# Plain keys and queries transposed as four 64x64 pieces at a time, into two PSUM banks

## The chip, the cores and the metric

The kernel runs on one NeuronCore of a Trainium2 chip. Its engines each follow their own instruction stream: TensorE (PE in the profile; its weight loads are listed apart as PEld), VectorE (DVE), ScalarE (ACT), GpSimd (POOL) and SyncE (SP). The last two issue most DMAs. The metric is the device time of one launch in microseconds; lower is better. Before the change it is 304.22 us, the median of three runs from 304.19 to 305.46.

## What is computed

Attention over a batch of 8, with 8 heads, 576 positions and 64 numbers a head, and behind it a two-layer network on the 4608 tokens. The first four heads ("plain") look back over a window of 32 positions, the last four ("dilated") over 128 positions, every fourth one.

```python
scores = scale * np.matmul(q, k.transpose(0, 1, 3, 2))
mask_plain = (rel >= 0) & (rel < window)
mask_dil = (rel >= 0) & (rel < window * dilation) & (rel % dilation == 0)
...
attn = np.exp(scores)
attn = attn / (np.sum(attn, axis=-1, keepdims=True) + 1e-09)
out = np.matmul(attn, v)
...
x = attn_out.transpose(0, 2, 1, 3).reshape(B * S, H * D)
h = x @ w_in
g = h * (1.0 / (1.0 + np.exp(-beta * h)))
return g @ w_out
```

Here `rel` is the query's position less the key's, and `w_in` is 512 by 2048.

## The kernel before, in words

**Tiles.** TensorE contracts over the partitions, so keys and queries are needed with the 64 numbers of a head on the partitions: two heads fill 128. The heads thus go in pairs: `x` counts the two plain pairs (`kT[kv][:, x]`, `qT[kv][:, x]`), and head `h` of a pair lies on partitions 64h to 64h+63. The scores of a head are 64-row matmuls on its half (L728), the exponentials go from a PSUM bank into `pt` (L600), multiplied by a mask from batch 1 on (L604), and `pt` is the stationary operand of the value matmuls (L785). The results are normalised on DVE (L619, L620), transposed back (L822, L837, L807) and copied into `xT`. The network works on blocks of 512 tokens: first layer (L868), tanh on ACT (L877), gate on DVE (L882), second layer (L903), eviction (L918, L920), store.

**Where keys and queries come from.** For batches 0, 1 and 2 (`b < DIRECT`) they are loaded position by position and transposed on TensorE; from batch 3 on a DMA transposes them. For the plain heads the staging tile `stp[z]` (`z` 0 for keys, 1 for queries) holds the heads of pair `i`: row 64h + g has nine consecutive positions of head h. One step, named KP0, KP1, QP0 or QP1, transposes one pair: 18 pieces of 64x64 (L473), piece (j, h) from rows of half h to partitions of half h, all into one bank. Then one copy of 128x576 on DVE or ACT (L239) empties the bank into `kT` or `qT`. The dilated steps KD0 to QD1 transpose six blocks of 96x128 each (L466).

**The order of the work** is made when the program is built. `Plan.op` notes every step with its engines, an estimated duration, the steps it needs and a due time `vt`. `Plan.run` then simulates the engines: on each it takes the step that could start first and, among those within 40 to 60 ns of the first (`NEAR`), the one with the earliest due time. A step that needs PSUM takes one of 8 banks (`acquire`), or several at once; `CAPS` limits how many of a kind are open. The instructions are emitted in that order, and each engine keeps to it whatever the chip does. Where the simulation sees TensorE idle it puts in a matmul of zeros as filler (L1015). `NUDGE` moves single steps by hand: its keys are the numbers of the steps in the order in which they are noted, and the value (ns) is added to the step's start when the first is chosen; -900 means that it is taken well ahead of its turn.

Step numbers that matter below: 4 is the zeroing of `pt` and `ptt` (DVE, L317), 7 is `add_d` (POOL, L346: the additive mask of the dilated heads of batch 0), 13 the load of the first keys on SP, 16 to 18 the other loads of keys and queries of batch 0 on POOL, 32 is `ident_f` (POOL, L948), which the transpose of beta (step 33, L951) needs. `add_d` is needed by the four 128x512 matmuls at L654, which start the dilated scores of batch 0.

In `attention`, a pair's transposes and copy are these lines:

```python
g = Group("a")
tr = plan.op([("PE", (18 * mm(64) if kind == "P" else 6 * mm(QT)))],
             lambda e, g=g, z=z, kind=kind, i=i: t_transposes(g, z, kind, i),
             srcs + [ident], vt, acquire=g)
...
steps[n] = [plan.op([dve(S), act(S)], evac, [tr, fill1] + war(key), vt, group=g)]
```

Of the kernel before, what the change touches and what calls it, by code (L numbers as in the profile page):

```python
# [9 lines left out]
BF16 = mybir.dt.bfloat16  # L10
# [26 lines left out]
class Plan:  # L37
# [3 lines left out]

    CAPS = {"h": 3, "p": 4, "o": 2, "z": 4, "a": 8, "s": 5, "w": 6}
    SWITCH = 95
    NUDGE = {32: -900, 54: 400, 98: -900, 188: -60, 192: -150, 263: -400, 287: 400, 292: -400, 294: 60,
        296: -150, 299: -60, 313: 900, 338: -400, 369: -150, 403: 400, 411: 900, 424: 400, 427: -150,
        527: -400, 770: -150, 970: -900, 977: -900, 988: -400, 1057: -60}
    LAT = {"PE": 210, "ACT": 45, "DVE": 45, "POOL": 60, "SP": 0}
    NEAR = {"PE": 40, "ACT": 60, "DVE": 60, "POOL": 60, "SP": 0}

# [3 lines left out]
    def op(self, engs, fn, deps=(), vt=0.0, acquire=None, group=None, dma=0, lat=None, halves=False, sbuf=False):  # L53
        acquire = acquire if acquire is None or isinstance(acquire, list) else [acquire]
        o = Op(engs, fn, deps, vt, acquire, group or acquire, dma, lat, halves, sbuf)
        o.bias = self.NUDGE.get(len(self.ops), 0)
        self.ops.append(o)
# [123 lines left out]
def kernel(  # L181
# [10 lines left out]
    nc = tc.nc  # L192
    P = 128
    B, H, S, D = q.shape
# [11 lines left out]
    GD = S // RD  # L206
    RP = 9
    GP = S // RP
    QT = 96
# [6 lines left out]
    DIRECT = 3  # L216
# [14 lines left out]
    plan = Plan(range(8))  # L231
    E = {"ACT": nc.scalar, "DVE": nc.vector, "POOL": nc.gpsimd}

    def bank(g, dt=FP32):
        b = BANKS[g.bank][:]
        return b if dt == FP32 else b.bitcast(BF16)

    def copy(e, out, in_):
        (nc.scalar.copy if e == "ACT" else E[e].tensor_copy)(out=out, in_=in_)  # L239
# [4 lines left out]
    ident_b = const([P, P], BF16, "ident_b")  # L244
# [28 lines left out]
    st = [const([P, 2 * RD * D + 2 * RP * D], BF16, f"st{i}") for i in range(2)]  # L273
    std = [s[0:2 * GD, 0:2 * RD * D].rearrange("p (x e) -> p x e", x=2) for s in st]
    stp = [s[:, 2 * RD * D:].rearrange("p (x e) -> p x e", x=2) for s in st]
# [16 lines left out]
    mm = lambda n: n / 2.4 + 2.5  # L292
# [14 lines left out]
    ident = plan.op([("POOL", 550)], t_ident, vt=-8.985)  # L307
# [150 lines left out]

    def t_transposes(g, z, kind, i):
        if kind == "D":
            tp = bank(g, BF16)[:, 0:S].rearrange("p (s x g) -> p s x g", s=3, x=2)
            for s_ in range(3):
                for x in range(2):
                    nc.tensor.transpose(tp[:, s_, x], std[z][:, x, (2 * s_ + i) * P:(2 * s_ + i + 1) * P],  # L466
                                        ident_b[0:2 * GD, 0:2 * GD])
        else:
            tp = bank(g, BF16)[:, 0:S].rearrange("p (j g) -> p j g", j=RP)
            for j in range(RP):  # L470
                for h in range(2):
                    rows = slice(64 * h, 64 * h + 64)
                    nc.tensor.transpose(tp[rows, j], stp[z][rows, i, j * D:(j + 1) * D], ident_b[rows, rows])  # L473

    def at_once(x, i, h):

# [5 lines left out]
    def war(*keys):  # L482
        return [o for key in keys for o in last.get(key, ())]

    def used(key, o):
        last.setdefault(key, []).append(o)

    def wrote(*keys):
        for key in keys:
            last[key] = []  # L490
# [38 lines left out]
    def attention(b, ld, names, vts):  # L529
# [2 lines left out]
        vt_of = dict(zip(names, vts))  # L532
        kv = b % 2
        if b < DIRECT:
            for n in [x for x in names if x[0] in "KQ"]:
                z, kind, i = "KQ".index(n[0]), n[1], int(n[2])
                vt = vt_of[n]
                g = Group("a")
                srcs = ld["qk", z, 0 if kind == "P" else 4]
                srcs = srcs if isinstance(srcs, list) else [srcs]  # L540
                tr = plan.op([("PE", (18 * mm(64) if kind == "P" else 6 * mm(QT)))],
                             lambda e, g=g, z=z, kind=kind, i=i: t_transposes(g, z, kind, i),
                             srcs + [ident], vt, acquire=g)
                used(("st", z), tr)
                def evac(e, g=g, z=z, kind=kind, i=i):
                    tp = bank(g, BF16)[:, 0:S]
                    if kind == "P":
                        dst = qT[kv][:, i] if z else kT[kv][:, i, WIN:]
                        copy(e, dst.rearrange("p (g j) -> p g j", j=RP), tp.rearrange("p (j g) -> p g j", j=RP))
                    else:  # L550
                        copy(e, (dk, dq)[z][kv][:, i].rearrange("p h (g s) -> p h g s", s=3),
                             tp.rearrange("p (s h g) -> p h g s", s=3, h=4))
                key = (("kT", "qT")[z], kv, i) if kind == "P" else (("dk", "dq")[z], kv, i)
                steps[n] = [plan.op([dve(S), act(S)], evac, [tr, fill1] + war(key), vt, group=g)]
                wrote(key)
        else:
            ready = {"D": [ld["x", 0, 4], ld["x", 1, 4]], "P": [ld["x", 0, 0], ld["x", 1, 0], fill1]}
# [25 lines left out]
        vt = vt_of["zVAL"]  # L583
# [41 lines left out]
        for name in [n for n in names if n[0] in "ST"]:  # L625
            vt = vt_of[name]
            if name == "T":
                g = Group("s")

                def score(e, g=g):  # L630
                    sc = bank(g)[:, 0:256].rearrange("p (c h r u) -> p h c r u", h=4, c=2, r=2)
                    for h4 in range(4):
# [4 lines left out]
                              deps, vt, acquire=g)  # L637
# [7 lines left out]
            x = int(name[1])  # L645
# [3 lines left out]
            gs = [Group("s") for _ in range(2 * len(xs))]  # L649
            if x >= 2:  # L650
# [7 lines left out]
                def score(e, xs=xs, gs=gs):  # L658
                    for n, x in enumerate(xs):
                        for i in range(4):  # L660
                            r, h4 = i // 2, 2 * (x - 2) + i % 2
                            for c in range(2):
# [7 lines left out]
                              acquire=None if before else gs, group=gs, halves=True)  # L670
# [9 lines left out]
            j = int(name[2])  # L680
            if b >= AT_ONCE:
                if name != "S00":
                    continue
                gs = [Group("w") for _ in range(6)]
# [37 lines left out]
            def score(e, xs=xs, j=j, gs=gs):  # L722
                for n, x in enumerate(xs):
                    for a in range(3):
                        i = 3 * j + a
                        for h in range(2):
# [7 lines left out]
                          vt, acquire=None if before else gs, group=gs, halves=True)  # L734
# [3 lines left out]
            for n, x in enumerate(xs):  # L738
                for h in range(2):
                    exp_and_mask((x, j, h), sop, gs[2 * n + h], vt, 3 * QT,  # L740
                                 lambda g=gs[2 * n + h]: bank(g)[:, 0:3 * QT].rearrange("p (a n) -> p a n", a=3),
                                 lambda x=x, j=j, h=h: pt[x][:, 6 * j:6 * j + 6].rearrange(
                                     "p (a h) n -> p h a n", h=2)[:, h, :, 0:QT],
                                 lambda j=j: mask_n[:, 1 + j:4 + j],
                                 [("pt", x, i) for i in range(3 * j, 3 * j + 3)])
        for name in [n for n in names if n[0] in "VU"]:
            vt = vt_of[name]
            g = Group("a")
# [14 lines left out]
            x, j = int(name[1]), int(name[2])  # L763
# [37 lines left out]
        for name in [n for n in names if n[0] in "XY" and b < BY_DMA]:  # L801
            vt = vt_of[name]
            x = int(name[1])
            g = Group("a")
# [28 lines left out]
            j = int(name[2])  # L833
# [124 lines left out]
    vts = [-3 + 2 * i / len(first) for i in range(len(first))] + [-3, -2.5]  # L958
    vts[first.index("T"):len(first)] = [.2,.35,.45,.5]
    attention(0, ld[0], names0, vts)  # L960

    def xready(lo, hi, kts=range(NKT)):
# [34 lines left out]
    for t in range(NTT):  # L997
# [4 lines left out]
        b = t + 1  # L1002
# [46 lines left out]
```

The softmax here doesn't subtract the row's maximum and nothing guards it: scores larger than these inputs give would overflow.

## Time and profile before

| | |
|---|---|
| time, median of 3 | 304.22 us (304.19 to 305.46) |
| profiled execution: span, first to last instruction | 302.8 us (the page lists no other time of this execution) |
| PE busy | 292.8 us, 97% |
| DVE, ACT, POOL busy | 187.8, 170.3, 88.5 us |
| L473, plain transposes, 216 pieces of 64x64 | busy 4.7 us, one lasts 194 ns; at 10.5 to 13.0, 31.4 to 32.7 and 54.8 to 58.3 us |
| L239, 128x576 copies out of a bank | one lasts about 0.75 us on DVE, 0.64 us on ACT |
| L868 and L903, the network's matmuls of 128x512 | 134.7 and 132.9 us busy |

Matmuls are pipelined: one that lasts 194 ns may be followed by the next some ns later, so what a group costs is read from the times at which runs start. A view in order of time has the start, the busy time, the engine, the line, what is written from what, the shapes, how many, and in brackets how long the engine sat idle before it and for whom. A few matmul records are missing in any trace, so that three listed may be four.

### The profile page before, as it was taken

The page shows a single profiled execution, that of the slowest core. Times are in us where ns is not written, and L with a number is a line of the kernel's source. Part 1 is how long each engine was busy: PE and PEld are TensorE (multiplying, and loading weights), DVE is VectorE, ACT ScalarE, POOL GpSimd, SP SyncE. Part 2 cuts the span into 40 slices and gives each one's busy share as a digit, 9 for nine tenths or more (in the row PEclk, how much of TensorE's full clock was granted, in tenths as well). Part 3 has the DMA queues.
Part 4 walks back from the last instruction along what each step waited for, and adds up shares of the span by engine and source line. Part 5 has one row for each costly group of instructions (what it writes and reads, how often), then busy time and mean ns, then how long its engine had stood idle before and what let it go on. Part 6 is the DMA issues. An engine that isn't in the chain of part 4 may idle for free.

```text
span 302.8 us, 5972 instructions
## 1 busy us (share of the span) xinstructions
PE 292.8 (97%) x2271; PEld 150.7 (50%) x2307; DVE 187.8 (62%) x424; ACT 170.3 (56%) x306; POOL 88.5 (29%) x126
## 2 busy tenths in 40 slices
PE   7989999999999999999999999999999999999995
PEld 4756555544554444445544454455544444444454
DVE  4777877688867837777677467577746544343300
ACT  3658974856745737383476447646465544554411
POOL 8997263762236137200631055200000000000000
PEclk9999999999999999999999999999999999999999
DMA  7999999799769999995699989996160100010122
GB/s 161 182 209 202 206 177 211 140 133 176 197 153 190 181 213 168 179 187 130 107 189 164 160 208 184 144 212 163 27 167 1 37 36 35 35 37 35 52 86 71
DMA packets 111248, 41.98 MB, mean 139 GB/s; under 512 B 87620, under 2 KB 104596, under 8 KB 111220
## 3 DMA queue, kind: packets, MB, share of 16 engines
q0 software_dynamic: 60336, 18.58, 58.7%
q1 hardware_dynamic: 50740, 22.95, 35.5%
q8 instruction: 18, 0.29, 0.4%
q10 hardware_dynamic: 144, 0.07, 0.1%
q14 instruction: 10, 0.08, 0.1%
HBM read 37.76 MB, written 18.87 MB: 187 GB/s over the span
## 4 chain that ended last, share of the span: by engine, by line
PE 89%; DVE 6%; issue 2%; DMA 1%; ACT 0%; SPq 0%; DVEq 0%
PE bank L903 40%; PE bank L868 39%; DVE g L882 2%; PE bank L785 2%; DMA beta_row<-in_moe_beta_dram 1%; PE bank L664 1%; PE bank L769 1%; PE bank L692 1%; PE bank L466 1%; PE bank L473 1%; DVE xdm L620 1%; DVE ptt L604 1%; PE bank L654 1%; PE bank L754 1%; PE bank L728 1%
## 5 line engine op out<-in xcount | busy, mean ns | idle before, releaser
L877 ACT ACTIVATE tnh<-bank,beta_half 128x512 bf16<-128x512 f32 x144 | 97.6, 690 | 71.4 <-PE bank L868 68.6
L903 PE MATMUL bank<-w_out_bf,g 128*128 128x512 bf16 (+2 forms) x588 | 136.2, 367 | 1.6 <-issue 0.8
L868 PE MATMUL bank<-xT,w_in_bf 128*128 128x512 bf16 (+1 forms) x568 | 136.1, 376 | 1.0 <-issue 0.2
L882 DVE SCALAR_TENSOR_TENSOR g<-tnh,bank 128x512 bf16<-128x512 bf16 x144 | 97.3, 686 | 62.2 <-ACT tnh L877 61.4
L868 PEld LDWEIGHTS <-w_in_bf 128*128 128x128 bf16 x584 | 55.4, 98 | 61.8 <-issue 0.4
L903 PEld LDWEIGHTS <-g 128*128 128x128 bf16 x608 | 54.9, 98 | 56.5
L918 ACT ACTIVATE osb<-bank 128x512 f32<-128x512 f32 (+1 forms) x34 | 20.0, 588 | 31.2 <-PE bank L903 30.4
L600 ACT ACTIVATE pt<-bank 128x384 bf16<-128x384 f32 (+1 forms) x54 | 20.4, 466 | 6.4 <-PE bank L692 4.3
L604 DVE TENSOR_TENSOR pt<-pt,mask_n 128x384 bf16<-128x384 bf16 (+1 forms) x41 | 15.1, 381 | 8.7 <-ACT pt L600 8.1
L600 ACT ACTIVATE ptd<-bank 128x512 bf16<-128x512 f32 x32 | 16.6, 602 | 6.6 <-PE bank L664 6.6
L620 DVE TENSOR_TENSOR xsp<-bank,rcp 96x384 bf16<-96x384 f32 x32 | 17.7, 554 | 1.1
L619 DVE RECIPROCAL rcp<-bank 128x4 f32<-128x4 f32 (+2 forms) x72 | 12.8, 178 | 6.6 <-PE bank L785 3.4
L390 POOL DMA_DIRECT2D vp<-in_v_dram x9 | 15.3, 1696 | 0.4 <-DVE dkt L239 0.4
L620 DVE TENSOR_TENSOR xdm<-bank,rcp 128x256 bf16<-128x256 f32 x32 | 13.6, 425 | 1.1
L390 POOL DMA_DIRECT2D s<-in_q_dram x10 | 13.6, 1356 | 0.0
L390 POOL DMA_DIRECT2D vt<-in_v_dram x16 | 13.4, 1007 | 0.2 <-issue 0.2
L920 DVE TENSOR_SCALAR osb<-bank 128x512 f32<-128x512 f32 (+2 forms) x4 | 2.1, 522 | 18.1 <-PE bank L903 18.1
L604 DVE TENSOR_TENSOR ptd<-ptd,mask_d 128x512 bf16<-128x512 bf16 x27 | 10.8, 422 | 2.2 <-ACT ptd L600 1.7
L981 POOL COPY pace<-xT 1x2 bf16<-1x2 bf16 x4 | 0.9, 213 | 38.0 <-DMA xT<-x 38.0
L239 POOL COPY vd<-st 128x1024 bf16<-128x1024 bf16 x5 | 5.3, 1053 | 22.3 <-DMA st<-in_v_dram 22.3
L390 POOL DMA_DIRECT2D s<-in_k_dram x10 | 11.1, 1115 | 1.0 <-issue 0.8
L785 PEld LDWEIGHTS <-pt 128*128 128x128 bf16 x192 | 8.8, 97 | 4.7
(110 smaller groups left out, 188.2 us busy)
## 6 DMA issues: line engine op xcount, KB each, us to landing
out_dram<-osb SPq DMA_DIRECT2D x35, 256.0 KB, 3.4
s<-in_q_dram POOLq DMA_DIRECT2D x10, 288.0 KB, 9.4
s<-in_k_dram POOLq DMA_DIRECT2D x10, 288.0 KB, 6.5
w_out_bf<-in_moe_w_out_dram POOLq DMA_DIRECT2D x2, 1024.0 KB, 16.8
vp<-in_v_dram POOLq DMA_DIRECT2D x7, 288.0 KB, 17.1
st<-in_q_dram POOLq DMA_DIRECT2D x6, 288.0 KB, 9.8
x<-xsp SPq DMA_DIRECT2D x12, 144.0 KB, 4.5
st<-in_k_dram POOLq DMA_DIRECT2D x5, 288.0 KB, 11.2
```

The source lines that it names most:

```text
L239: (nc.scalar.copy if e == "ACT" else E[e].tensor_copy)(out=out, in_=in_)
L390: {"POOL": nc.gpsimd, "SP": nc.sync}[queue].dma_start(out=out, in_=in_)
L600: nc.scalar.activation(out=w(), in_=sc(), func=ACT.Exp, scale=SCALE)
L604: E[e].tensor_tensor(out=w(), in0=w(), in1=m(), op=ALU.mult)
L619: nc.vector.reciprocal(out=r, in_=p[..., D])
L620: nc.vector.tensor_tensor(out=dst, in0=p[..., 0:D], in1=r.unsqueeze(len(p.shape) - 1).to_broadcast(list(p.shape[:-1]) + [D]), op=ALU.mult)
L785: nc.tensor.matmul(pv[:, a, h2, :], lhsT=lhs, rhs=vp[kv][:, (2 * x + h2) * NI + 3 * j + a, 0:D + 1], start=True, stop=True)
L868: nc.tensor.matmul(bank(g)[:, a:z], lhsT=w_in_bf[:, kt, fb * P:(fb + 1) * P], rhs=xT[:, kt, xo + a:xo + z], start=(i == 0 and kt == kts[0] ...
L877: nc.scalar.activation(out=th[:, 0:n], in_=bank(g)[:, 0:n], func=ACT.Tanh, scale=beta_half[:, fb:fb + 1])
L882: nc.vector.scalar_tensor_tensor(out=g_t[t % 2][:, fb, c0:c0 + n], in0=th[:, 0:n], scalar=1.0, in1=bank(g)[:, 0:n], op0=ALU.add, op1=ALU.mult)
L903: nc.tensor.matmul(bank(g)[:, lo:hi], lhsT=g_t[t % 2][:, fb, tb * P:(tb + 1) * P], rhs=w_out_bf[:, fb, lo:hi], start=(fb == 0), stop=(fb = ...
L918: nc.scalar.mul(out=ob[:, lo:hi], in_=bank(g)[:, lo:hi], mul=0.5)
```

## The change

The two plain pairs of a batch's keys (and of its queries) are transposed in one step of 36 pieces, which takes two banks. For each j there are four pieces: pair 0's two heads go to their own halves of the first bank, and pair 1's two heads to the other half each (`half[h ^ x]`) of the second bank. So the four pieces of a j use the four combinations of source half and destination half. Pair 1's heads therefore lie on swapped halves in `kT` and `qT`; the scores pair them alike, and the exponentials write each head's block to its old place in `pt` (`h ^ x`). The two copies stay, one for each bank, and both now need the one step. The estimate of its duration is 648 ns; the two steps it replaces had 18 `mm(64)` each, where `mm(n)` is n/2.4 + 2.5 ns. There are two steps fewer for each of three batches, so later steps have other numbers, and the table `NUDGE` is another one altogether.

```diff
-    NUDGE = {32: -900, 54: 400, 98: -900, 188: -60, 192: -150, 263: -400, 287: 400, 292: -400, 294: 60,
-        296: -150, 299: -60, 313: 900, 338: -400, 369: -150, 403: 400, 411: 900, 424: 400, 427: -150,
-        527: -400, 770: -150, 970: -900, 977: -900, 988: -400, 1057: -60}
+    NUDGE = {4: 900, 7: -900, 66: -900, 191: -60, 196: -900, 217: 400, 242: 150, 268: -60, 270: -400,
+        271: -900, 272: -60, 341: 60, 361: 60, 424: 150, 475: -900, 481: -150, 523: 150, 527: 400,
+        528: 900, 547: -900, 548: -900, 559: -400, 663: 900, 788: 60, 819: -400, 1120: -900}
...
+    def t_quarters(gs, z):
+
+        tps = [bank(g, BF16)[:, 0:S].rearrange("p (j g) -> p j g", j=RP) for g in gs]
+        half = [slice(64 * h, 64 * h + 64) for h in range(2)]
+        for j in range(RP):
+            for x in range(2):
                 for h in range(2):
-                    rows = slice(64 * h, 64 * h + 64)
-                    nc.tensor.transpose(tp[rows, j], stp[z][rows, i, j * D:(j + 1) * D], ident_b[rows, rows])
+                    nc.tensor.transpose(tps[x][half[h ^ x], j], stp[z][half[h], x, j * D:(j + 1) * D],
+                                        ident_b[half[h], half[h]])
...
+                if kind == "P" and i == 0:
+                    gs = [Group("a") for _ in range(2)]
+                    tr = plan.op([("PE", 18 * 36)], lambda e, gs=gs, z=z: t_quarters(gs, z),
+                                 srcs + [ident], vt, acquire=gs)
+                    quarters[z] = gs, tr
+                    used(("st", z), tr)
...
+                if kind == "P":
+                    g, tr = quarters[z][0][i], quarters[z][1]
...
-                                     "p (a h) n -> p h a n", h=2)[:, h, :, 0:QT],
+                                     "p (a h) n -> p h a n", h=2)[:, h ^ (x if b < DIRECT else 0), :, 0:QT],
```

More of the change, by code (lines that the diff above doesn't have):

```diff
@@ L457, in crossbar, with t_transposes @@
                        deps, vt, dma=288 * 1024 / .2 / 1000, lat=5500 if b == DIRECT else 6500)
[L461 to L470, printed above, removed]
+    def t_transposes(g, z, i):
+        tp = bank(g, BF16)[:, 0:S].rearrange("p (s x g) -> p s x g", s=3, x=2)
+        for s_ in range(3):
+            for x in range(2):
+                nc.tensor.transpose(tp[:, s_, x], std[z][:, x, (2 * s_ + i) * P:(2 * s_ + i + 1) * P],
+                                    ident_b[0:2 * GD, 0:2 * GD])
+    def t_quarters(gs, z):
+        tps = [bank(g, BF16)[:, 0:S].rearrange("p (j g) -> p j g", j=RP) for g in gs]
+        half = [slice(64 * h, 64 * h + 64) for h in range(2)]
+        for j in range(RP):
+            for x in range(2):
                 for h in range(2):
-                    rows = slice(64 * h, 64 * h + 64)
-                    nc.tensor.transpose(tp[rows, j], stp[z][rows, i, j * D:(j + 1) * D], ident_b[rows, rows])
+                    nc.tensor.transpose(tps[x][half[h ^ x], j], stp[z][half[h], x, j * D:(j + 1) * D],
+                                        ident_b[half[h], half[h]])
     def at_once(x, i, h):
@@ L534, in attention @@
         if b < DIRECT:
+            quarters = {}
             for n in [x for x in names if x[0] in "KQ"]:
@@ L537, in attention @@
                 vt = vt_of[n]
-                g = Group("a")
                 srcs = ld["qk", z, 0 if kind == "P" else 4]
                 srcs = srcs if isinstance(srcs, list) else [srcs]
[L541 to L544, printed above, removed]
+                if kind == "P" and i == 0:
[4 more added lines that the diff above has]
+                    used(("st", z), tr)
+                elif kind == "D":
+                    g = Group("a")
+                    tr = plan.op([("PE", 6 * mm(QT))], lambda e, g=g, z=z, i=i: t_transposes(g, z, i),
+                                 srcs + [ident], vt, acquire=g)
+                    used(("st", z), tr)
+                if kind == "P":
+                    g, tr = quarters[z][0][i], quarters[z][1]
                 def evac(e, g=g, z=z, kind=kind, i=i):
```

## The prediction, made before the changed kernel was run

> **What bounds the kernel now.** I read the page first, then the busy time by stretch, then the chain of waits, then the order of time where the changed lines run.
>
> ```profile
> PE 292.8 (97%) x2271; PEld 150.7 (50%) x2307; DVE 187.8 (62%) x424; ACT 170.3 (56%) x306; POOL 88.5 (29%) x126
> ```
>
> ```profile
> 0.00:20.00 20.00, 16.63 (x232) 11.80 (x234) 13.27 (x45) 10.55 (x23) 17.80 (x37) 1.00 1.18 180
> 20.00:60.00 40.00, 39.00 (x475) 22.73 (x481) 30.32 (x71) 29.77 (x62) 22.95 (x35) 1.00 1.31 189
> 60.00:100.00 40.00, 39.06 (x321) 19.80 (x325) 31.47 (x74) 23.68 (x46) 17.66 (x22) 1.00 1.32 171
> 100.00:200.00 100.00, 98.99 (x687) 48.45 (x698) 67.06 (x153) 58.96 (x102) 30.13 (x36) 1.00 1.35 171
> ```
>
> The columns behind the stretch are its length and the busy time of PE, PEld, DVE, ACT and POOL. There are two regimes. From 20 us on PE is the bound: between 20 and 200 us it is idle for 1.00 + 0.94 + 1.01 = 2.95 us, part of that missing records. There, PE time saved is time saved, unless what follows waits for something else. Before 20 us PE is partly idle or on fillers, and a chain of waits sets when the dense part begins:
>
> ```profile
> 1.28 4.33 DMA beta_row<-in_moe_beta_dram
> ...
> 5.74 0.26 PE bank L951
> 6.00 1.82 PE bank L654 x4
> 7.81 0.97 PE bank L466 x12
> ...
> 8.81 0.77 DVE dk L239
> ```
>
> The first link is not a key or a query but the load of beta: its transpose (L951) stands in PE's queue ahead of the four added masks (L654), and these ahead of the first key transposes (L466). The keys were ready earlier:
>
> ```profile
> 5.45 0.83 ACT L239 CAST st<-g 96x768 bf16<-96x768 f32 x1 [3.15 <-DMA g<-in_k_dram]
> ...
> 5.93 1.89 PE L654 MATMUL bank<-add_d,ident_b 128*128 128x512 bf16 x4
> 7.61 1.17 PE L466 MATMUL bank<-ident_b,st 96*128 96x96 bf16 x12
> ```
>
> The cast ends at 5.45 + 0.83 = 6.28; the transposes start at 7.61.
>
> The lines that the change edits, in batch 2:
>
> ```profile
> 54.79 0.47 PE L473 MATMUL bank<-ident_b,st 64*64 64x64 bf16 x18
> 55.19 1.04 PE L868 MATMUL bank<-xT,w_in_bf 128*128 128x512 bf16 x3
> 56.16 0.76 PE L473 MATMUL bank<-ident_b,st 64*64 64x64 bf16 x36
> 56.85 1.04 PE L868 MATMUL bank<-xT,w_in_bf 128*128 128x512 bf16 x4
> 57.81 0.47 PE L473 MATMUL bank<-ident_b,st 64*64 64x64 bf16 x18
> 58.22 0.62 PE L664 MATMUL bank<-dq,dk 64*128 64x128 bf16 x16
> ```
>
> The 18 pieces hold PE for 55.19 - 54.79 = 0.40 us, the 36 for 0.69, so 18 pieces cost 0.29: 16 ns a piece, 32 ns the two of a j. The fixed part behind a run is 0.40 - 0.29 = 0.11. Ahead of one, four L868 matmuls hold 57.81 - 56.85 = 0.96 where four take 0.86 in the chain of waits: 0.10. So each separate run costs 0.21 beside its pieces.
>
> **The change part by part.** The sum is made against the profiled execution's span of 302.8; the median of the runs is 1.4 above it, and I carry the difference over to the median.
>
> *The pieces.* 36 transposes a step replace 2 x 18; the number of instructions is the same, and only overlap can save. No row shows two pieces with the same source rows and different destinations side by side. Bound from above: they take turns, 2 x 32 = 64 ns for four, no saving. Bound from below: all four run together. A single matmul of 65 columns follows the last one by 30 ns (six of L785 last 0.34 us, one 0.19: 0.15/5), two together take 32, so each further piece adds some 2 to 3 ns and four take about 37. I take 37, the row being two pieces on different rows at almost the price of one. That is 27 ns for each of 18 fours a batch: 0.49 us a batch. In batch 2 it lies on PE's path: -0.5, ends 0 and -0.5. In batch 1 something else is late next:
>
> ```profile
> 31.36 1.32 PE L473 MATMUL bank<-ident_b,st 64*64 64x64 bf16 x72
> 31.87 0.76 DVE L239 COPY kT<-bank 128x576 bf16<-128x576 bf16 x1 [0.17 <-PE bank L473]
> ...
> 32.85 0.40 PE L664 MATMUL bank<-dq,dk 64*128 64x128 bf16 x8 [0.16 <-ACT kT L239]
> ...
> 33.40 0.40 PE L664 MATMUL bank<-dq,dk 64*128 64x128 bf16 x8 [0.15 <-DVE g L882]
> ```
>
> Behind the 72 pieces PE already waits for ACT and DVE, which empty the banks. With the first copy not earlier, 0.49 saved turns into 0.49 more waiting unless the new order puts a matmul there. I take half: -0.25, ends 0 and -0.5.
>
> *Weight loads, where a rule speaks against this.* In the trace the 18 weight loads at 54.79 take 0.36 us beside their 18 pieces' 0.47; with only two groups of source rows, each load runs while a piece of its own rows is still in flight. The Trainium skill ("TensorE: Matmul & The Clock Gate", Part 3, What overlaps and what doesn't) says that a weight load overlaps with running matmuls only when its row group differs. By that rule pieces sharing rows would take turns, the pieces would save nothing, and the sum would be -1.1 instead of -1.85; the row contradicts it for loads of the same tile, and no row shows two tiles on the same rows.
>
> *Fewer runs.* Batch 2 has three runs (18, 36, 18). Two steps make at most two: one run less is -0.2, ends 0 and -0.4 (both steps adjacent).
>
> *The copies.* Twelve of 128x576 before and after, 0.75 on DVE or 0.64 on ACT. The first of a pair now waits for 36 pieces instead of 18: 9 x 37 = 0.33 against 0.29, nothing if the pieces overlap, 0.29 later if not. The second comes earlier. Hidden by L868 matmuls from batch 1 on; in batch 0 it lies on the chain twice, +0.1, inside the next term. The swapped index of the exponentials changes an offset, not a shape: 0.
>
> *The prologue.* Step 32 (`ident_f`) is no longer taken first, so beta's transpose comes late and no longer stands ahead of L654. Step 7 (`add_d`) is taken first on POOL. Its three instructions take 4.32 to 5.26 today; in front they end near 1.8. The identity, which L654 also reads, ends at 2.92 today and is pushed back by 0.94 less the 0.4 of `ident_f`: 3.5. L654 then runs from 3.6 to 5.3, in place of fillers, before the keys are cast. L466 can start at 6.28 + 0.1 instead of 7.61: -1.2. What is pushed back on POOL's queue: the loads of the dilated queries (1.53), plain keys (2.88) and plain queries (3.60), by some 0.5 each; the values' loads behind them are not, since `add_d` no longer stands there. The rate by stretch (500 KB in 2 to 4 us, 370 in 4 to 6) brings the 576 KB of keys and 288 of dilated queries by 6 us, and at 196 GB/s plain keys by 7.5, queries by 9, values by 10.4 and 12. With 0.5 added: 6.5, 8, 9.5 and 12.5 against needs that are 1.2 earlier: 7.6, 9.3, 11.0 and 13.0 (the halo copy, 14.23 now). These are estimates, and the last has 0.5 to spare. SP's queue is unchanged. The delayed zeroing of `pt` (step 4, 0.68 of DVE at 1.52) is not needed before the first exponential at 11.92: 0. From 8.81 to 19.8 the chain is mostly DVE, which shifts as a whole. I take -0.9, ends 0 (another load late) and -1.2.
>
> *The rest of the order.* Twenty-odd other nudges move; the views say nothing of them. A gain is limited by PE's idle time of 2.95 between 20 and 200, of which the one large wait is 0.51 (L728 at 65.98). I take 0, ends -0.6 and +2 (four such waits).
>
> Sum: -0.5 - 0.25 - 0.2 - 0.9 = -1.85; 304.22 - 1.85 = **302.4**, span 300.9.
>
> **The rivals.**
> 1. *The four pieces take turns.* For: no row shows them together. The pieces save nothing: -0.9 - 0.2 = -1.1, 303.1.
> 2. *The prologue's gain is given back.* A load of batch 0 comes later than estimated, or the batch-1 work that starts earlier waits for its loads; DMA is busy throughout 4 to 50 us. For: 0.5 to spare is little. -0.95, 303.3.
> 3. *Two banks at once.* A step that needs two banks waits until a second is free, with PE's matmuls queued behind. Price at most one copy, 0.76, for each of four steps from batch 1 on: 302.4 + 3.0 = 305.4. Against: in batch 1 the four banks are there today within 1.3 us.
> 4. *Changing the destination half drains PE* (the other side). Going from 64x64 to another tile shape costs 0.10 each way above. If pieces of the swapped pair count as another shape, each four pays twice: 36 fours from 20 us on x 0.19 = +6.8, and the pieces save nothing: 304.2 - 1.1 + 6.8 = 310. It decides from (1.1 + 1.5)/36 = 72 ns a four. Against: two tiles of the same shape alternate at 16 ns today. The Trainium skill ("TensorEngine Tiling (Array Packing)", Key Properties) has the drain only for a change of mode, not of tile.
>
> **How the numbers follow.** 0.5% is 1.5 us, about what a measurement of this kernel can tell from no change. Forecast: 0.42, own range 301.0 (all terms at their better ends: -1.2 - 1.0 - 0.4 - 0.6 = -3.2) to 302.9. Rival 1: 0.17. Rival 2: 0.13. Rival 3: 0.15, half of it above 305.7 where waits of the new order add to it. Rival 4: 0.13. Faster: 0.42. Same: 0.17 + 0.13 + 0.07 = 0.37. Slower: 0.08 + 0.13 = 0.21. The range runs from 301.0 to 305.9 and leaves out rival 4 and a little at either end.
>
> **What would show it.** Right: a run of 36 pieces holds PE for about 0.11 + 0.33 = 0.44 us (0.69 if they take turns, over 2 if they drain); L654 starts near 3.6 and L466 near 6.4; the first L868 starts near 18.9 instead of 19.77; batch 2 has two runs. Wrong: L466 at 7.6 or the first L868 at 19.8 (prologue), idle time ahead of the new runs for a copy (banks), more than 3 us of PE idle between 20 and 200 (order).

## The result and the profile after

The changed kernel takes 305.62 us (median of 20 executions, 303.59 to 306.65) where the kernel before took 304.30 beside it (20 executions, 303.81 to 305.46): a ratio of 1.0027, interval 1.0015 to 1.0038. The forecast was 302.4; the time lies inside its range, on the other side of no change. The profiled execution is the slowest of the 20 (306.65, span 304.9); where that matters below, it is said. Two later executions, one of 307.66 us (padded copy earlier) and one of 306.38 (padded copy on ACT), count as slow and are left out of the ratios and medians below; neither was traced.

Busy time of the engines, and then the stretches with the columns of before (length, PE, PEld, DVE, ACT, POOL, granted clock, DMA share, GB/s):

```profile
PE 295.2 (97%) x2309; PEld 148.5 (49%) x2309; DVE 187.7 (62%) x421; ACT 170.5 (56%) x305; POOL 89.2 (29%) x130
```

```profile
0.00:20.00 20.00, 15.93 (x247) 10.49 (x248) 12.89 (x46) 11.05 (x24) 17.56 (x37) 0.96 1.16 175
20.00:60.00 40.00, 39.83 (x478) 21.94 (x476) 30.28 (x68) 28.57 (x59) 23.77 (x35) 0.98 1.31 190
60.00:100.00 40.00, 37.59 (x296) 18.41 (x295) 30.42 (x70) 23.87 (x46) 18.22 (x24) 0.96 1.31 167
100.00:200.00 100.00, 100.00 (x715) 48.75 (x714) 69.65 (x157) 58.77 (x102) 29.70 (x37) 1.00 1.37 172
```

From 100 to 200 us PE never stops. Between 60 and 100 us it is idle for 2.41 us, and the granted clock is 0.96. Here is the place, PE alone in order of time, behind the two new runs of 36 pieces:

```profile
54.95 0.48 PE L475 MATMUL bank<-ident_b,st 64*64 64x64 bf16 x36
55.36 1.04 PE L881 MATMUL bank<-xT,w_in_bf 128*128 128x512 bf16 x4
56.32 0.48 PE L475 MATMUL bank<-ident_b,st 64*64 64x64 bf16 x36
56.73 1.90 PE L881 MATMUL bank<-xT,w_in_bf 128*128 128x512 bf16 x8
58.47 1.03 PE L916 MATMUL bank<-w_out_bf,g 128*128 128x512 bf16 x4
59.43 0.62 PE L677 MATMUL bank<-dq,dk 64*128 64x128 bf16 x16
62.46 0.28 PE L646 MATMUL bank<-qt,dkt 128*128 128x64 bf16 x4 [2.41 <-DVE g L895]
62.57 1.60 PE L916 MATMUL bank<-w_out_bf,g 128*128 128x512 bf16 x4
63.97 1.91 PE L881 MATMUL bank<-xT,w_in_bf 128*128 128x512 bf16 x4
```

L646 (L633 before) scores the last rows of the dilated queries, which are copied into `qt`, padded, by two small DVE copies a batch (L239). The same time on DVE and POOL:

```profile
56.32 0.24 DVE L239 COPY qt<-dq 64x128 bf16<-64x128 bf16 x1
...
57.23 1.63 POOL L390 DMA_DIRECT2D s<-in_q_dram  x1
...
58.23 3.45 DVE L239 COPY qt<-dq 64x128 bf16<-64x128 bf16 x1
...
58.34 1.70 POOL L390 DMA_DIRECT2D vp<-in_v_dram  x1
...
59.51 2.15 POOL L390 DMA_DIRECT2D s<-in_k_dram  x1
```

Two copies of one shape: 0.24 us at 56.32, and 3.45 at 58.23. The second began while POOL issued batch 3's loads, one long issue overlapping the next, and it ended at 58.23 + 3.45 = 61.68, as the third of them did (59.51 + 2.15 = 61.66). On DVE the gate (`g`) stood behind it, and PE waited for that.

The wait is followed by a slower clock. Stretches of 2 us, last columns granted clock, DMA share, GB/s:

```profile
60.00:62.00 2.00, 0.05 (x2) 0.07 (x1) 1.97 (x2) 1.97 (x4) 2.00 (x4) 1.00 1.94 161
62.00:64.00 2.00, 1.54 (x9) 0.64 (x9) 2.00 (x6) 0.38 (x1) 1.08 (x2) 0.72 2.44 156
64.00:66.00 2.00, 2.00 (x10) 0.90 (x9) 0.54 (x3) 0.02 (x1) 0.00 (x0) 0.50 1.76 165
66.00:68.00 2.00, 2.00 (x18) 0.98 (x16) 1.27 (x4) 1.35 (x2) 0.00 (x0) 0.93 2.32 160
```

So the clock is halved for some 3.4 us (1.12, 2.00 and 0.28 us of these stretches), which costs 1.7. At a clock of 0.50 four L881 matmuls last 1.91 us instead of 1.03. In 6 of the 20 executions the mean clock over the whole was 0.999 or 1.000, and they took 303.59 to 304.58; in the other 14 it was 0.994 or 0.989, and they took 305.15 to 306.65. The profiled one, at 0.989, has a second such stretch at 18 to 22 us; where the others have theirs was not traced.

### The profile page after: what moved, and what is told of

Read it like the earlier page. It is cut to its first block, busy times and chain, and to the rows that moved or that the text cites. A ratio compares the mean times of both kernels' runs of the same rounds, so it can differ in the third digit from the quotient of the medians.

```text
span 304.9 us, 6012 instructions
## 1 busy us (share of the span) xinstructions
PE 295.2 (97%) x2309; PEld 148.5 (49%) x2309; DVE 187.7 (62%) x421; ACT 170.5 (56%) x305; POOL 89.2 (29%) x130
## 4 chain that ended last, share of the span: by engine, by line
PE 90%; DMA 5%; DVE 3%; ACT 1%; POOL 0%; issue 0%; POOLq 0%; DVEq 0%; ACTq 0%
PE bank L916 41%; PE bank L881 40%; DMA st<-in_k_dram 3%; DMA st<-in_q_dram 2%; PE bank L798 2%; DVE qt L239 1%; PE bank L782 1%; PE bank L705 1%; PE bank L465 1%; PE bank L677 1%; DVE g L895 1%; PE bank L767 1%; PE bank L741 1%; DVE dq L239 1%; PE bank L646 0%
## 5 line engine op out<-in xcount | busy, mean ns | idle before, releaser
L916 PE MATMUL bank<-w_out_bf,g 128*128 128x512 bf16 (+2 forms) x608 | 140.8, 369 | 0.0
L881 PE MATMUL bank<-xT,w_in_bf 128*128 128x512 bf16 (+1 forms) x584 | 140.6, 380 | 0.0
L881 PEld LDWEIGHTS <-w_in_bf 128*128 128x128 bf16 x584 | 55.7, 99 | 62.4 <-issue 1.9
L633 DVE TENSOR_TENSOR xsp<-bank,rcp 96x384 bf16<-96x384 f32 x32 | 17.7, 554 | 1.1
L617 DVE TENSOR_TENSOR pt<-pt,mask_n 128x384 bf16<-128x384 bf16 (+1 forms) x37 | 13.2, 386 | 5.9 <-ACT pt L613 5.7
L390 POOL DMA_DIRECT2D vp<-in_v_dram x9 | 14.4, 1598 | 0.4 <-DVE g L895 0.4
L633 DVE TENSOR_TENSOR xdm<-bank,rcp 128x256 bf16<-128x256 f32 x32 | 13.6, 424 | 1.1
L390 POOL DMA_DIRECT2D s<-in_q_dram x10 | 12.6, 1256 | 0.0
L390 POOL DMA_DIRECT2D s<-in_k_dram x10 | 12.2, 1220 | 1.0 <-issue 0.9
L617 POOL TENSOR_TENSOR pt<-pt,mask_n 128x288 bf16<-128x288 bf16 x9 | 6.4, 727 | 15.0 <-ACT pt L613 15.0
L798 PE MATMUL bank<-vp,pt 128*128 128x65 bf16 x192 | 10.1, 195 | 0.3 <-DMA vp<-in_v_dram 0.2
```

Source lines behind the costliest of these rows:

```text
L390: {"POOL": nc.gpsimd, "SP": nc.sync}[queue].dma_start(out=out, in_=in_)
L617: E[e].tensor_tensor(out=w(), in0=w(), in1=m(), op=ALU.mult)
L633: nc.vector.tensor_tensor(out=dst, in0=p[..., 0:D], in1=r.unsqueeze(len(p.shape) - 1).to_broadcast(list(p.shape[:-1]) + [D]), op=ALU.mult)
L798: nc.tensor.matmul(pv[:, a, h2, :], lhsT=lhs, rhs=vp[kv][:, (2 * x + h2) * NI + 3 * j + a, 0:D + 1], start=True, stop=True)
L881: nc.tensor.matmul(bank(g)[:, a:z], lhsT=w_in_bf[:, kt, fb * P:(fb + 1) * P], rhs=xT[:, kt, xo + a:xo + z], start=(i == 0 and kt == kts[0] ...
L916: nc.tensor.matmul(bank(g)[:, lo:hi], lhsT=g_t[t % 2][:, fb, tb * P:(tb + 1) * P], rhs=w_out_bf[:, fb, lo:hi], start=(fb == 0), stop=(fb = ...
```

## The experiments

All have five rounds of timing (4 to 12 executions) beside the kernel before, whose median was 304.30 beside the first four, 304.31 beside the next four, 304.68 beside the four after, 304.45 beside the last two. Compare ratios, then, rather than times. In these kernels the steps are emitted in the order that the planner made, with single steps moved: `MOVE = [([n], m)]` puts step n right behind step m on every queue, `BANK` sets the banks that a step takes, and `FILL` puts matmuls of zeros ahead of a step. Line numbers shift by up to 31.

| kernel | time, median | ratio | interval |
|---|---|---|---|
| changed kernel | 305.62 | 1.0027 | 1.0015 to 1.0038 |
| new order, old pieces | 304.18 | 1.0007 | 0.9994 to 1.0019 |
| old order, new pieces | 304.73 | 1.0009 | 0.9996 to 1.0023 |
| before with the prologue's order alone | 304.25 | 1.0006 | 0.9997 to 1.0015 |
| changed, padded copy earlier | 301.39 | 0.9921 | 0.9895 to 0.9947 |
| the same with old pieces | 301.81 | 0.9923 | 0.9911 to 0.9935 |
| changed, padded copy on ACT | 301.34 | 0.9908 | 0.9893 to 0.9922 |
| changed, both copies on ACT | 302.61 | 0.9937 | 0.9916 to 0.9959 |
| the same with old pieces | 302.10 | 0.9918 | 0.9902 to 0.9934 |
| changed, padded copy as a maximum | 302.20 | 0.9921 | 0.9906 to 0.9937 |

**The change taken apart: new order with old pieces.** The order of the changed kernel stays; only the pieces go back to their own halves.

```diff
-nc.tensor.transpose(tps[x][half[h ^ x], j], stp[z][half[h], x, j * D:(j + 1) * D],
+nc.tensor.transpose(tps[x][half[h], j], stp[z][half[h], x, j * D:(j + 1) * D],
...
-    h=2)[:, h ^ (x if b < DIRECT else 0), :, 0:QT]
+    h=2)[:, h, :, 0:QT]
```

> The changed kernel with its order untouched, but each step's 36 pieces transposed as before, each head to its own half (and the exponentials' index set back). Theory (the pieces gain, the new order loses): a run of 36 pieces holds PE for 0.69 us instead of 0.41, 0.28 more for each of the four runs behind 20 us; 305.6 + 1.1 = 306.7 us. Rival (the swapped pieces themselves disturb what follows): not slower than the changed kernel, 305.6 or less.

Measured: 304.18, below the changed kernel. The theory's number failed: taking the faster pieces away cost nothing. The held copy is still there (2.91 us at 57.45, to the end of the third long issue at 60.34), but counted from the start of POOL's chain PE reaches the wait 0.55 us later, about what two runs with old pieces take longer, and it stands 1.86 us instead of 2.41. Only 2 of 12 executions have a mean clock of 0.994. The other 10 have a median of 304.2, the 6 of the changed kernel at full clock 303.8: the difference between the two kernels goes with the clock and is not shown to be the pieces'.

**Old order with new pieces.**

```diff
+    def t_quarters(gs, z):
+        ...
-    lambda e, ...: t_transposes(g, z, kind, i),
+    lambda e, ...: t_transposes(g, z, kind, i) if kind == "D" else
+                   t_quarters(quarters[z], z) if i == (b < 2) else None,
...
+    MOVE = [([392], 306)]
+    BANK = {389: [1], 391: [7]}
```

> The kernel before with its order kept step by step, except that the 36 pieces of keys (and of queries) are transposed at one place, four at a time on swapped halves; in batch 2 one run less. Theory (the pieces gain, the new order loses): four runs behind 20 us save 0.28 each and one run less saves 0.2, of which batch 1 loses some 0.3 again to its copies: 304.3 - 1.0 = 303.3 us. Rival (the swapped pieces disturb what follows): 304.3 or more.

The 36 pieces run at the second pair's place in batches 0 and 1 and at the first's in batch 2; the exponentials have the changed index.

Measured: 1.0009, no gain. The time that the pieces save is waited for a few lines on: 0.60 and 0.34 us ahead of the dilated scores of batch 1 (31.83 and 32.80; 0.16 and 0.15 before), 0.29 ahead of those of batch 2 (57.86; none before).

**The held copy moved.** In the changed kernel's order, batch 2's second padded copy (step 389) comes right behind the first.

```diff
+    MOVE = [([389], 388)]
```

> The changed kernel with one DVE step moved: batch 2's second copy of the padded dilated queries (3.45 us at 58.23 instead of 0.19) stands right behind the first one, ahead of the loads that POOL issues from 57.2 us on. Theory (that copy is held up by POOL's issue of loads, and TensorE waits 2.4 us for it and then runs 3.4 us at half clock): the copy lasts 0.2, the wait ahead of L646 goes, the granted clock stays at 1.00 between 60 and 68 us; 305.6 - 2.4 = 303.2 us or better. Rival (something else on DVE holds up these matmuls): the wait moves to the next step, 305.6.

Measured: 301.39, faster than either kernel. The wait is gone; all engines of the run with the early copy:

```profile
55.17 0.45 DVE L257 COPY qt<-dq 64x128 bf16<-64x128 bf16 x2
...
58.36 2.15 POOL L408 DMA_DIRECT2D s<-in_k_dram  x1
...
58.83 0.29 PE L664 MATMUL bank<-qt,dkt 128*128 128x64 bf16 x4
```

Two copies take 0.45, and L664 (L646 above) runs with no idle time in brackets.

**Batch 1's key transposes put back.** Steps 205, 209 and their copies 206, 210 behind step 121 (the first network matmuls).

```diff
+    MOVE = [([205, 209, 206, 210], 121)]
```

> The changed kernel with one group moved: the transposes of batch 1's dilated keys and their copies stand behind the first four L881 matmuls instead of ahead of batch 0's last but one value matmuls. Theory (they stand in TensorE's queue at 18.6 us and wait for a load that lands at 19.0, with batch 0's end behind them): the first L881 starts at about 19.0 instead of 20.31; 305.6 - 1.2 = 304.4 us, less if the clock no longer drops at 18 to 22 us. Rival (batch 0's end is bound by DVE or by the values' load at 15.5): first L881 at 20 or later, 305.6.

Measured: 1.0018 (0.9998 to 1.0039), the first network matmul at 19.43. In the other traces of the new order but that of the changed kernel it comes at 18.79 to 19.70 with the keys where the changed kernel has them, so that place isn't what sets it. The wait at L646 stays (2.40 us), but here no slower clock follows:

```profile
62.00:64.00 2.00, 2.00 (x14) 1.00 (x13) 1.92 (x7) 0.56 (x2) 0.35 (x1) 1.00 2.44 157
64.00:66.00 2.00, 1.95 (x17) 1.03 (x16) 1.65 (x4) 1.28 (x3) 0.00 (x0) 1.00 1.64 139
```

This execution took 304.52 us.

**The prologue alone.** The kernel before, with only the steps of the prologue moved: `add_d` first on POOL, `ident_f` late, the added masks (55, 59) ahead of the keys' transposes, beta's transpose (33, 34) behind them.

```diff
+    MOVE = [([7], 13), ([32], 8), ([55, 59], 18), ([33], 47), ([34], 48)]
+    BANK = {33: [7]}
```

> The kernel before, old pieces, with the prologue's order alone changed as in the new kernel: add_d first on POOL, ident_f behind add_p, the four L654 matmuls ahead of the last seven fillers, beta's transpose behind the plain keys. My prediction's term: the first L466 at 6.4 instead of 7.61, the first L868 at 18.9 instead of 19.77, 304.3 - 0.9 = 303.4 us. Theory after the first runs (later loads and ACT give half of it back): first L466 at 6.1, first L868 at 19.3, 303.8 us. Rival (all of it given back): 304.3 us.

Measured: 1.0006. The network starts 1.24 us earlier than in the trace of before, and PE waits 1.13 us for batch 1's keys. PE of that run:

```profile
18.53 1.09 PE L886 MATMUL bank<-xT,w_in_bf 128*128 128x512 bf16 x3
...
26.68 0.43 PE L484 MATMUL bank<-ident_b,st 96*128 96x96 bf16 x6 [1.13 <-DMA st<-in_k_dram]
```

But the trace of before is a late one. The old prologue is also in the kernel with the old order and new pieces, whose PE shows:

```profile
5.77 1.04 PE L685 MATMUL bank<-add_d,ident_b 128*128 128x512 bf16 x4
6.65 0.68 PE L484 MATMUL bank<-ident_b,st 96*128 96x96 bf16 x12
...
18.37 1.09 PE L899 MATMUL bank<-xT,w_in_bf 128*128 128x512 bf16 x3
```

The four added masks hold PE for 6.65 - 5.77 = 0.88 us here and for 7.61 - 5.93 = 1.68 in the trace of before, where PE still ran at half the pace: the traces have the full clock recorded from 3.88 us on here and from 9.98 there (the clock column reads 1.00 where nothing is recorded). So a network start at 18.5 is not shown to be the new prologue's doing.

**The early copy with the old pieces.**

```diff
-nc.tensor.transpose(tps[x][half[h ^ x], j], ...
+nc.tensor.transpose(tps[x][half[h], j], ...
+    MOVE = [([389], 388)]
```

> The changed kernel with the one copy moved ahead (as in the run that took 301.8 us) and with the old pieces, each head on its own half. Theory (the pieces' gain was swallowed by the wait for that copy, and counts once the wait is gone): 0.28 us for each of the four runs behind 20 us, 301.8 + 1.1 = 302.9 us. Rival (the pieces gain nothing on the path): 301.8 us.

Measured: a ratio of 0.9923 against 0.9921 with the new ones: no difference, though the wait is gone. The profiled execution of this kernel happened to be its slowest (304.42), and shows a second victim:

```profile
55.32 1.63 POOL L408 DMA_DIRECT2D s<-in_q_dram  x1
...
55.69 4.31 DVE L257 COPY vd<-vd 128x1024 bf16<-128x1024 bf16 x1 [0.83 <-DMA vd<-in_v_dram]
...
57.60 2.15 POOL L408 DMA_DIRECT2D s<-in_k_dram  x1
...
61.31 0.62 PE L695 MATMUL bank<-dq,dk 64*128 64x128 bf16 x16 [3.17 <-DVE g L913]
```

The copy that spreads batch 2's values (0.41 us in the changed kernel) waited for its load, began inside the same chain of issues and was held 4.31 us, to 60.00, shortly behind the end of the third (59.75). Here it was the landing of a load that decided which copy was caught.

**The copy on ACT.**

```diff
-                copy(e, qt[kv][rows, c]...
+                copy("ACT" if (b, c) == (2, 1) else e, qt[kv][rows, c]...
```

> The changed kernel, its order untouched, with batch 2's second copy of the padded dilated queries on ACT instead of DVE. Theory (DVE's copy is held up by the loads that POOL issues beside it; ACT's is not): the copy takes about 0.25 us at the same place, no wait ahead of L646, 302 us. Rival (its operand or its place holds it up on any engine): still over 2 us and 305.6.

Measured: 301.34, as with the early copy. The copy took 0.29 us.

**Fillers in the wait.** 18 matmuls of zeros ahead of batch 2's L646, to keep the clock up.

```diff
+    FILL = {400: [3] * 18}
```

> The changed kernel with 18 fillers of zeros (128x256, 1.9 us at full clock) ahead of the L646 matmuls that wait 2.4 us; the wait itself stays. Theory (behind the idle time the clock halves for 3.4 us in most executions, which costs 1.7): granted clock 1.00 between 62 and 66 us in the profile, the times close together at 303.7 us. Rival (the idle time alone is the cost, the clock is not): 305.6 us or more.

Measured: 307.77, 1.0110 (1.0081 to 1.0139). In the profiled execution the values' copy was held (4.29 us at 55.70), so PE waited at the scores ahead of the fillers (3.73 us at 61.30), and the fillers ran behind the wait for 3.64 us. The mean clock was below 0.995 in 5 of 6, and in the trace it fell to 0.50 again (0.66 at 62 to 64 us, 0.50 at 64 to 66). Whether fillers inside the wait keep the clock up was thus not tested; the run shows that a filler at a fixed place is no cure for a wait that moves.

**Both copies on ACT, with new and with old pieces.**

```diff
+                copy("ACT" if (b, c) in [(2, 1)] else e, qt[kv][rows, c]...
+            copy("ACT" if b in [2] else e, vd[kv][:, :, :, 0:D], vd16_of[b])
```

> The changed kernel with two copies of batch 2 on ScalarE: the padded queries' second copy and the copy that spreads the values (128x1024). In the runs before this one either of them was held for 2.9 to 4.3 us on VectorE while GpSimd issued its chain of loads, and whichever it was, TensorE waited 2.0 to 3.7 us some 2 to 4 us later. Theory: it is any VectorE copy from SBUF to SBUF that begins within that chain, so with both gone nothing in batch 2 is held, no TensorE wait over 0.6 us stands between 55 and 66 us, and the time is 301.2 (300.8 to 301.8) in every execution, none over 303. Rival A, the hold passes to the next VectorE instruction, whatever it is: a wait of 2 us stays and the time is 303.5 to 305.6. Rival B, ScalarE's longer copy (some 1.1 us for 1024 elements against 0.41) and its wait for the values' load delay the tanh behind it: 302.2.

> The same two copies on ScalarE, with the old 64x64 transposes (both pieces of a pair on one half) and the old halves for the heads: all of the changed order without the pieces. Theory, pieces worth nothing because waits for copies stand right behind them: within 0.25 us of the run with the new pieces, 301.0 to 301.5. Rival, now that no wait of the kind stands behind them their 0.75 us is seen: 301.9 to 302.0.

Measured: 302.61 and 302.10. No wait over 0.6 us stands there any more (0.52 at 59.34 at most), but the times are not as steady as expected (301.89 to 305.69 with the new pieces; the traced one, 304.53, waits 1.13 us for a mask at 141.51 instead), and the ratios are no better than with one copy moved. The pieces again gain nothing. Now it can be seen where their time goes. Batch 1 with old pieces and both copies on ACT:

```profile
31.00 0.76 PE L475 MATMUL bank<-ident_b,st 64*64 64x64 bf16 x36
31.68 0.40 PE L677 MATMUL bank<-dq,dk 64*128 64x128 bf16 x8
32.01 0.76 PE L475 MATMUL bank<-ident_b,st 64*64 64x64 bf16 x36
32.70 0.40 PE L677 MATMUL bank<-dq,dk 64*128 64x128 bf16 x8
```

and with new ones, in the run with the maximum described below (there L475 is the pieces' line too, and L681 is the L677 of the others):

```profile
31.06 0.48 PE L475 MATMUL bank<-ident_b,st 64*64 64x64 bf16 x36
31.47 0.40 PE L681 MATMUL bank<-dq,dk 64*128 64x128 bf16 x8
31.80 0.48 PE L475 MATMUL bank<-ident_b,st 64*64 64x64 bf16 x36
32.93 0.40 PE L681 MATMUL bank<-dq,dk 64*128 64x128 bf16 x8 [0.65 <-DVE g L899]
```

Each run is 0.27 to 0.28 us shorter, and the second scores wait 0.65: they start 1.70 us after the first pieces with the old ones, 1.87 with the new. In two other traces it is 1.84 with old pieces (early copy) and 1.82 with new ones (both copies on ACT): no gain here, and no steady loss.

**Batch 1's padded copy on ACT too.**

```diff
+                copy("ACT" if (b, c) in [(1, 1), (2, 1)] else e, qt[kv][rows, c]...
```

> As the first, and batch 1's second padded-query copy on ScalarE too: on VectorE it was stretched from 0.19 to 0.57 to 0.79 us at 30 to 31 us, and TensorE waited 0.43 to 0.77 us for the instruction behind it at about 32.3 us. Theory: that wait shrinks by some 0.4 us, 300.8. Rival, the wait is the dilated scores' own for the activation and is refilled: no difference, 301.2.

Measured: 302.37, ratio 0.9934 (0.9914 to 0.9954), no difference. The padded copy of that batch that stays on DVE takes 0.78 us at 31.09 instead of 0.19, and PE still waits 0.52. In the run with both copies on ACT it was also the first of the two that was held (0.75, the second 0.19), so it is not shown that the hold passed on: the copy that was moved may not have been the held one.

**Form or place.** The same instruction, at the same place on DVE, as the maximum of the operand with itself; the values' copy on ACT.

```diff
-                copy(e, out, in_)
+                if (b, c) == (2, 1):
+                    nc.vector.tensor_tensor(out=out, in0=in_, in1=in_, op=ALU.max)
+                else:
+                    copy(e, out, in_)
```

> The values' copy of batch 2 on ScalarE, and the padded queries' second copy where the changed kernel has it, on VectorE and at the same place, but written as the maximum of the operand with itself (a tensor_tensor) in place of a copy. Theory: only the copy form is held up beside GpSimd's issues (four tensor_tensor masks ran at their usual 0.47 us beside them): it takes about 0.2 us, no wait ahead of the dilated tail scores, 301.3. Rival, the place is what matters and any VectorE instruction there is held: it takes about 3 us, TensorE waits 2 us and the time is 303.6 to 305.6.

Measured: 302.20, ratio 0.9921. All engines:

```profile
57.62 1.70 POOL L390 DMA_DIRECT2D vp<-in_v_dram  x1
...
58.48 0.22 DVE L587 TENSOR_TENSOR qt<-dq 64x128 bf16<-64x128 bf16 x1
...
59.62 0.28 PE L650 MATMUL bank<-qt,dkt 128*128 128x64 bf16 x4 [0.30 <-DVE g L899]
```

Inside the same chain of issues the copy took 3.45 us (from the first issue on; 2.91 in the new order with old pieces, where it began in the second, as the maximum does) and the maximum takes 0.22: beside these issues it is the form of the instruction. It is not the form alone. In the kernel before, a DVE mask, a tensor_tensor too, takes 1.91 us instead of 0.28 beside a mask on POOL:

```profile
61.97 2.10 POOL L604 TENSOR_TENSOR ptd<-ptd,mask_d 128x512 bf16<-128x512 bf16 x1
62.32 1.91 DVE L604 TENSOR_TENSOR ptt<-ptt,mask_t 96x256 bf16<-96x256 bf16 x1
```

The Trainium skill ("SBUF — State Buffer", Who interferes with whom) says that copies can run in a mode that needs the port pair shared with GpSimd, that the second to come is blocked for the whole instruction of the first, and that a tensor_tensor has no such mode but with both inputs in SBUF contends with GpSimd's reads, which agrees with both rows; it warns of the descriptor writing that a copy blocks. Here it is the other way round, the copy blocked by the issues, and held beyond the one in flight, to the end of the third. The port itself is not seen in any row, and no run moved the issues: that they are the cause is read from the ends of the held copies beside theirs.

**What makes the prologue count.** The prologue's moves again, with batch 1's load of dilated keys ahead of two `w_in` loads on POOL as in the new order; and that load alone.

```diff
+    MOVE = [([7], 13), ([32], 8), ([55, 59], 18), ([33], 47), ([34], 48), ([198], 47)]
...
+    MOVE = [([198], 47)]
```

> The kernel before, with the old pieces, the changed kernel's prologue order and one more move: batch 1's load of dilated keys is issued on GpSimd ahead of the second and third load of w_in, as the changed order has it (issued at about 10 us there, at 12.4 behind them in the run with the prologue alone). With the prologue alone TensorE started the first network matmul 1.24 us earlier (18.53) and then stood 1.13 us for these keys' load at 26.68. Theory: the early load is the other half of the prologue's gain; the wait at 26.7 goes and the time is 1.1 us below the prologue alone, 1.1 us below before: ratio 0.996. Rival: the gain is given back to the next wait, for the copies behind the pieces at 32 to 33 us, or the w_in loads come 0.65 us later and the network's matmuls wait for them: ratio 1.000.

> The kernel before with that load's place changed alone. Theory: TensorE did not wait for these keys before (two fillers stand there, the transposes begin at 26.62), so nothing is gained: ratio 1.000 (0.999 to 1.001). Rival: the w_in loads behind it come later and the start of the network is put off: ratio 1.002 or more.

Measured: 1.0012 (1.0002 to 1.0022) and 0.9992 (0.9982 to 1.0003). With both, the network starts at 18.07, 1.70 us earlier than in the trace of before, but with the load alone, behind the old prologue, it starts at 18.19. With both, the wait passes from the keys to the values:

```profile
26.39 0.68 PE L772 MATMUL bank<-vt,ptt 96*128 96x65 bf16 x8 [0.83 <-DMA vt<-in_v_dram]
```

Another load bounds the same place. The whole new order, with old pieces and the copy out of the way, gains some 2.4 us; which of its moves bring that was not found, only that the pieces don't, that the prologue and this load don't bring it alone, and that the two together don't.

## Why the prediction was wrong, point by point

**The step that failed.** The sum was -0.5 - 0.25 - 0.2 - 0.9, with 0 for the rest; measured is +0.8 us (0.0027 of 304.3). The largest term, "I take -0.9" for the prologue, is worth nothing (alone 1.0006, at best 0.9997), and so are the -0.75 of the pieces (in the old order 1.0009, at best 0.9996). "The rest of the order. ... I take 0" had neither of the two things that were there. With old pieces the whole order, prologue and all, is worth 1.0007 (0.9994 to 1.0019), where my terms for it came to -0.9 - 0.2 + 0; with the held copy out of the way it is worth -2.4 us (0.9923). So it holds a gain of 2.4 us, whose place was not found, and a loss of about as much, the held copy: a wait of 2.41 us, for which I had only rows of 0.51 as a measure, and a slower clock behind it, for which I had no term. That these cancel, and that the time lies inside my range, is luck: the upper end stands for waits for a second bank, with waits of the new order on top, and no wait for a bank was seen.

What the hold and the clock cost can be estimated from the medians: 301.4 without the hold, 303.8 in the 6 executions of the changed kernel whose clock stayed up, 305.7 in the 14 others. That makes 2.4 for the hold and 1.9 for the clock, if the 6 were held as the traced one was; the trace with a wait of 2.40 at full clock (304.52) supports it. The wait could not be found in the views of before: there this copy was not caught. That an instruction on DVE can be held beside POOL could have been read there, from the mask shown above: it stands in the chain of waits at 62.40 with 1.83 us. I read past it.

**The pieces: size right, effect wrong.** A run of 36 holds PE for 55.36 - 54.95 = 0.41 us (0.44 predicted). Less the 0.11 fixed, 0.30/9 = 33 ns for four, where I took 37: all four run together, on shared rows too. The rule of the Trainium skill that I weighed ("TensorE: Matmul & The Clock Gate", Part 3, What overlaps and what doesn't), by which a weight load overlaps only with another row group, is contradicted by these rows. But neither the 0.5 of batch 2 nor the 0.25 of batch 1 arrived: the old order with new pieces leaves room for 0.1 us at most (0.9996), and three pairs in the new order, with and without the pieces, show nothing clear of noise in their favour (ratios 0.9921 and 0.9923; 0.9937 and 0.9918; 1.0027 and 1.0007). I had the reason in batch 1, that PE then waits for the engines which empty the banks, and took half; all of it goes. In batch 2 I took PE's time for the path; beside the held copy it turned into waiting (2.41 us against 1.86 with old pieces). With both copies away the scores there wait 0.30 and 0.52 us in the runs with the new pieces and not at all in the one with the old; with one copy away they do not wait, and where the pieces' time goes then is not shown.

**One run fewer** is there (two runs in batch 2); its 0.2 was not measured apart. Of the copies' 0.1 nothing is seen apart either.

**The prologue: early rows right, gain not there.** Its rows in the changed kernel:

```profile
3.25 1.82 PE L667 MATMUL bank<-add_d,ident_b 128*128 128x512 bf16 x4
...
6.12 0.68 PE L465 MATMUL bank<-ident_b,st 96*128 96x96 bf16 x12 [0.28 <-ACT st L239]
...
7.56 0.68 PE L465 MATMUL bank<-ident_b,st 96*128 96x96 bf16 x12 [0.54 <-DMA st<-in_q_dram]
```

3.25 and 6.12 against 3.6 and 6.4 predicted; the load of the queries, delayed as expected, costs 0.54. The first network matmul comes at 20.31 in the changed kernel, in a stretch of slow clock, and at 18.53 with the prologue alone (18.9 predicted). But the -1.2 behind my term was read from one trace of before, in which the added masks ran at half the pace; in the traces of the old prologue at full pace L466 starts at 6.35 and 6.65 and the network at 18.19 and 18.37, and there was little left to gain. What did start earlier waited for batch 1's loads at 26 us. This second part is rival 2 in its second form ("the batch-1 work that starts earlier waits for its loads"), where I had given it 0.13; -0.9 should have been 0.

**The rivals.** 1, taking turns: no, 33 ns and not 64. 2: right as to the prologue. 3, two banks at once: no wait of the changed kernel is shown to be for a second bank, though its sum (305.4) is near the measured time for another reason. 4, draining: no. That a new wait would come with the order was in my list only as "waits of the new order".

## What to carry to other kernels

When an edit comes with a new order, the order is a change of its own: two runs, old work in the new order and new work in the old one, tell the two apart, and here the named change was worth nothing that could be measured and the order everything. Time saved on the bounding engine counts only as far as the engine that feeds its next matmul keeps up. Look for instructions that last far longer than the shortest of their shape: one copy at over ten times its usual length beside a chain of DMA issues on GpSimd cost a wait of 2.4 us, and another place, another engine or another form of the same instruction took it away; the best version here (the padded copy earlier or on ACT) is 0.8 to 0.9% below the kernel before. And read a start from more than one trace: the largest term of this forecast rested on one that was 1.4 us late.

## What the runs showed of the hardware that was not expected

- Copies on DVE from SBUF to SBUF can be held while GpSimd issues loads, to the end of an issue: 64x128 for 2.91 to 3.45 us instead of 0.19 and 128x1024 for 4.29 and 4.31 instead of 0.41 in the chain of long issues, 64x128 for 0.78 at 31.09 beside one issue of 1.18 that ended with it. Shorter issues hold less: 128x1024 took 0.74 at 14.57 in the kernel before, beside two of 0.68 and 0.67. Not every copy is held. In the kernel before, the values' copy took its usual time just behind the start of an issue of 1.70 us (56.30 to 58.00, the second of the two in the first row), and two of 64x128 took 0.20 and 0.19 at 115.55, beside issues of 1.34:

```profile
55.75 2.25 POOL L390 DMA_DIRECT2D s<-in_k_dram  x2
...
56.44 0.42 DVE L239 COPY vd<-vd 128x1024 bf16<-128x1024 bf16 x1
```

  What decides it was not found. A tensor_tensor of the same operands took 0.22 inside the chain; one beside POOL's own mask was held.
- After PE had been idle for 2.41 us its clock was granted at 0.50 for some 3.4 us, in the one execution of the changed kernel that was traced. Idle time alone does not decide it: 2.40 us (keys put back), 3.17 (early copy, old pieces) and 1.86 (new order, old pieces) were followed by a clock of 1.00. The Trainium skill ("TensorE: Matmul & The Clock Gate", HAM oscillation) gives a gap of some 3.4 us as what must be avoided; by these rows less can be too much. The clock's records in the traces point at where the idle time falls. The two slow stretches of the changed kernel's trace last 3.41 us each and begin 13 such lengths apart (18.50 and 62.88), so each trace can be cut into pieces of 3.41 us from its first rise of the clock. The idle time within one such piece was 2.41 and 2.39 us (changed kernel, fillers) where the clock fell at its end, and 1.66, 1.72 and 1.86 at most in the three where it did not. The drop at 18.50 follows only 0.89 us of idle time and does not fit; no run was made to test this reading.
- Four 64x64 transposes on the four combinations of row half and column half go through in 33 ns, where two on separate rows take 32.
